# A two-layer spectral and expert-lookup kernel: the last token tile in halves, with buffers of its own and first place in the plan, and products of constants on TensorE in planned pauses

## Chip, cores, metric

The kernel runs on one core of one Trainium2 chip. The metric is the device time of one execution in microseconds, as the median of several runs.

## What is computed

The input is `x`, 2048 tokens of 512 features, in fp32. Two kinds of layer alternate, twice each, with a layer norm ahead of each and a residual around it:

```python
x = x + _A_ref(_layernorm(x), dft_seq_re, dft_seq_im, dft_hid_re, dft_hid_im)
x = x + _B_ref(_layernorm(x), w_q, k1, k2, u, v)
x = x + _A_ref(_layernorm(x), dft_seq_re, dft_seq_im, dft_hid_re, dft_hid_im)
x = x + _B_ref(_layernorm(x), w_q, k1, k2, u, v)

# _A_ref: real part of a Fourier transform over hidden and sequence
a = einsum("bsd,ed->bse", x, dft_hid_re); b = einsum("bsd,ed->bse", x, dft_hid_im)
y = einsum("ts,bse->bte", dft_seq_re, a) - einsum("ts,bse->bte", dft_seq_im, b)

# _B_ref: per token and head (32), two score lists of 16 keys, best two of each,
# best two of their four sums pick 2 of 256 experts
s1 = einsum("nhd,ed->nhe", q1, k1); s2 = einsum("nhd,ed->nhe", q2, k2)
g = softmax(top_s); act = gelu(einsum("nd,nhkd->nhk", xf, u[top_e]))
out = einsum("nhk,nhk,nhkd->nd", g, act, v[top_e])
```

## The kernel before

The tokens are 16 tiles of 128. Each fp32 operand is split into a high and a low part (`xh`, `xl` and so on), and a product is three matmuls, high by high, high by low and low by high. A layer is cut into nine units: seven of 256 tokens and two of 128 (tiles 14 and 15). `seq_unit` sums the sequence transform of a unit over all 16 tiles in four `acc` banks of PSUM: DMA of a block of the matrix (`raw`, L411), ACT makes its high part (`ch`, L415), DVE the low one (`cl`, L419), PE multiplies (L453); at the end ACT and DVE take the sums out (`pth` L478, `ptl` L481). `token_tile` then does all the rest for one tile:

- the hidden transform (`y`, L519, 24 matmuls of 512 columns), the residual (L526), the norm (L216 to L228, with one step on GpSimd, and L237), transposes (L541) and the split (`th` L548, `tl` L552);
- the scores of both key lists against all heads (L569, 24 matmuls, taken out by L575 into `sc`) and the products with all experts (L587, then the gelu on ACT and DVE, L592 to L607);
- the top-two search on DVE (L633 to L683, `tree32`, `eq`, `codes`, `tree16`), the gates (L697 to L737), which end in the small tile `q`;
- transposes of `q` (L746, L750), selection matrices (`lr`, L767, L773), products of these (L784), taken out by L791 into the gate matrix; four DMAs write it to DRAM (`gdr`, L806) and two read it back in another order (`gt`, L813);
- gates times activations (L815), transposes (L823), split (L827, L831), product with `v` (L843), residual (L847), store (L849).

The order of all this is not the order of the code. Every step is recorded as an `Op` with an engine, a cost in microseconds from a small table, the steps it comes after, the buffers it takes, and a priority; `Plan.run` places the ops one by one at the earliest time at which engine, inputs and buffers are free, and among those of the same earliest time takes the smallest priority. The kernel then issues the instructions in the order of planned start. The engines execute their own instructions in that fixed order, with semaphores for what they wait for. The choice within one engine is

```python
first = min(t for t, _ in can)
t, o = min((c for c in can if c[0] <= first + 1e-9), key=lambda c: (c[1].prio, c[1].n))
```

and a tile's priority is `prio = (0, layer, at if at < len(units) - 1 else -1, i)`, where `at` is the place of its unit in the layer. In the second layer the last units are tiles 12 and 13 (one unit) and then tile 15. Of the buffers, `sc`, `eq`, `top`, `qt` and `gt` exist once, `lr` four times; the gate matrix takes the `sc` buffer too. The end of the program is therefore the chain of tile 15, beside what is left of tiles 12 and 13.

## Time and profile before

| | |
|---|---|
| median of 3 runs | 1291.42 us (1289.96 to 1292.18) |
| profiled execution | 1293.34 us, span of its instructions 1291.6 us |
| TensorE busy | 1240.4 us, 96% of the span |
| VectorE busy | 991.7 us, 77% |
| ScalarE busy | 468.5 us, 36% |
| mean granted TensorE clock | 0.986 |

The span counts from the first instruction to the last. A matmul's length in the timeline includes the time in which its columns run out of the array, so matmuls in a row overlap and the distance of their starts is what one costs. VectorE's instructions overlap a little as well where the next does not need the one before. "Idle before" names how long the engine had stood still and what it had waited for. The granted clock is TensorE's share of its full 2.4 GHz; the other level seen here is half of that, 1.2 GHz.

### The profile page before, as it was taken

The page shows a single profiled execution, that of the slowest core. Times are in us where ns is not written, and L with a number is a line of the kernel's source. Part 1 is how long each engine was busy: PE and PEld are TensorE (multiplying, and loading weights), DVE is VectorE, ACT ScalarE, POOL GpSimd, SP SyncE. Part 2 cuts the span into 40 slices and gives each one's busy share as a digit, 9 for nine tenths or more (in the row PEclk, how much of TensorE's full clock was granted, in tenths as well). Part 3 has the DMA queues.
Part 4 walks back from the last instruction along what each step waited for, and adds up shares of the span by engine and source line. Part 5 has one row for each costly group of instructions (what it writes and reads, how often), then busy time and mean ns, then how long its engine had stood idle before and what let it go on. Part 6 is the DMA issues. An engine that isn't in the chain of part 4 may idle for free.

```text
span 1291.6 us, 20342 instructions
## 1 busy us (share of the span) xinstructions
PE 1240.4 (96%) x7648; PEld 1026.8 (80%) x7648; DVE 991.7 (77%) x2226; ACT 468.5 (36%) x967; POOL 46.0 (4%) x71
## 2 busy tenths in 40 slices
PE   7999999999999999999999999999999999999972
PEld 6877778777788778899889887878878887888951
DVE  7899997888898959578883498684957669495774
ACT  6522244333333433243562343332333333332421
POOL 2010000000000000000000000000000000000000
PEclk9999999999999999999999999999999999999985
DMA  7866640322232332413454024242241414224012
GB/s 218 261 197 214 188 155 26 90 69 56 73 82 66 88 84 58 114 36 98 120 140 131 25 55 111 49 115 58 65 107 41 115 50 105 59 68 104 18 17 33
DMA packets 228291, 121.42 MB, mean 94 GB/s; under 512 B 140640, under 2 KB 206688, under 8 KB 228192
## 3 DMA queue, kind: packets, MB, share of 16 engines
q1 hardware_dynamic: 228192, 120.12, 34.8%
q8 instruction: 60, 0.98, 0.3%
q14 instruction: 39, 0.32, 0.1%
HBM read 107.50 MB, written 12.58 MB: 93 GB/s over the span
## 4 chain that ended last, share of the span: by engine, by line
PE 55%; DVE 19%; DMA 4%; issue 3%; ACT 2%; SPq 2%; POOL 0%; DVEq 0%; ACTq 0%
PE acc L453 24%; PE bank L569 11%; PE bank L519 10%; PE bank L843 3%; DVE cl L419 3%; DVE eq L624 2%; PE bank L587 2%; DMA gt<-gdr 2%; PE bank L453 2%; DMA gdr<-sc 2%; DVE lr L767 1%; DVE eq L656 1%; SPq L806 1%; DVE tmp L648 1%; DVE eq L672 1%
## 5 line engine op out<-in xcount | busy, mean ns | idle before, releaser
L453 PE MATMUL acc<-ch,xh 128*128 128x512 f32 (+1 forms) x1088 | 414.9, 381 | 8.0 <-ACT xh L244 7.8
L453 PE MATMUL acc<-cl,xh 128*128 128x512 f32 (+1 forms) x1088 | 404.7, 372 | 0.0
L453 PE MATMUL acc<-ch,xl 128*128 128x512 f32 (+1 forms) x1088 | 404.5, 372 | 0.0
L415 ACT CAST ch<-raw 128x512 fp32r<-128x512 f32 x256 | 158.6, 620 | 273.3 <-PE acc L453 242.4
L453 PEld LDWEIGHTS acc<-ch,xh 128*128 128x128 f32 x1088 | 205.7, 189 | 41.1 <-ACT xh L244 7.8
L453 PEld LDWEIGHTS acc<-cl,xh 128*128 128x128 f32 x1088 | 205.4, 189 | 36.4
L453 PEld LDWEIGHTS acc<-ch,xl 128*128 128x128 f32 x1088 | 205.9, 189 | 32.4 <-DVE xl L245 0.5
L419 DVE TENSOR_TENSOR cl<-raw,ch 128x512 fp32r<-128x512 f32 x256 | 174.9, 687 | 32.0 <-ACT ch L415 31.2
L569 PE MATMUL bank<-wh,tok 128*128 128x512 f32 x512 | 165.6, 394 | 1.0 <-ACT tok L548 0.7
L569 PEld LDWEIGHTS bank<-wh,tok 128*128 128x128 f32 x512 | 97.2, 190 | 22.4 <-ACT tok L548 1.1
L519 PE MATMUL bank<-dh,pth 128*128 128x512 f32 x256 | 101.3, 396 | 0.3 <-ACT sc L791 0.3
L519 PE MATMUL bank<-dh,ptl 128*128 128x512 f32 x256 | 100.0, 391 | 0.8 <-DVE ptl L481 0.8
L569 PE MATMUL bank<-wl,tok 128*128 128x512 f32 x256 | 100.6, 393 | 0.0
L519 PE MATMUL bank<-dl,pth 128*128 128x512 f32 x256 | 99.8, 390 | 0.0
L767 DVE TENSOR_TENSOR lr<-iota,qt 128x1024 f16<-128x1024 f16 x128 | 83.5, 685 | 17.0 <-ACT qt L750 16.9
L225 POOL TENSOR_TENSOR stats<-stats,half 128x1 f32<-128x1 f32 x64 | 44.7, 702 | 1193.7 <-DVE stats L222 1189.1
L633 DVE TENSOR_TENSOR tmp<-sc 128x512 f32<-128x512 f32 x32 | 22.0, 688 | 75.1 <-ACT sc L575 75.1
L624 DVE TENSOR_TENSOR eq<-sc,val 128x1024 f16<-128x1024 f32 x64 | 78.3, 1223 | 1.5
L575 ACT COPY sc<-bank 128x512 f32<-128x512 f32 x64 | 36.2, 590 | 112.1 <-PE bank L569 55.5
L478 ACT CAST pth<-acc 128x512 fp32r<-128x512 f32 x62 | 36.0, 586 | 91.1 <-PE acc L453 89.2
L481 DVE TENSOR_TENSOR ptl<-acc,pth 128x512 fp32r<-128x512 f32 x62 | 42.3, 687 | 33.0 <-ACT pth L478 33.0
L656 DVE TENSOR_TENSOR eq<-eq 128x512 f16<-128x512 f16 (+2 forms) x192 | 59.3, 309 | 1.6
(113 smaller groups left out, 1677.5 us busy)
## 6 DMA issues: line engine op xcount, KB each, us to landing
raw<-in_cseq SPq DMA_DIRECT2D x224, 256.0 KB, 2.8
wr<-in_wq SPq DMA_DIRECT2D x32, 512.0 KB, 3.9
raw<-in_ctile SPq DMA_DIRECT2D x32, 256.0 KB, 2.9
wr<-in_x SPq DMA_DIRECT2D x16, 256.0 KB, 3.8
row<-in_x SPq DMA_DIRECT2D x16, 256.0 KB, 3.3
gdr<-sc SPq DMA_DIRECT2D x128, 32.0 KB, 2.2
gt<-gdr SPq DMA_DIRECT2D x64, 64.0 KB, 2.9
x2d<-row SPq DMA_DIRECT2D x16, 256.0 KB, 2.1
```

Of the source, the lines that this page charges most:

```text
L225: nc.gpsimd.tensor_tensor(st[:, 1:2], st[:, 1:2], half, op=ALU.pow)
L415: nc.scalar.copy(t[1], t[0])
L419: nc.vector.tensor_sub(t[2], t[0], as32(t[1]))
L453: nc.tensor.matmul(target(d), w[:, s, d * P:(d + 1) * P], moving(s % per, part), start=(s == 0 and k == 0 and d % blocks == 0), stop=(s == ...
L481: nc.vector.tensor_sub(view(1, k, ds), acc[k], as32(view(0, k, ds)))
L519: nc.tensor.matmul(t["y"], w[:, k, c, t0:t0 + P], r[:, c, k, :], start=(k == 0 and c == 0 and m == 0), stop=(k == KD - 1 and c == 1 and m ...
L569: nc.tensor.matmul(t["pc", hf], w[:, k, :], r[:, k, hf], start=(m == 0), stop=(m == 3 * KD - 1))
L575: nc.scalar.copy(t["sc"][:, :, hf, :], t["pc", hf].rearrange("p h e -> p e h"))
L624: nc.vector.tensor_tensor(t["eq"], flat("sc"), t["val"][:, rank_][:, None, :].to_broadcast([P, E, 64]), op=ALU.is_equal)
L656: nc.vector.tensor_max(t["eq"][:, :m], t["eq"][:, :m], t["eq"][:, m:2 * m])
L767: nc.vector.tensor_tensor(t["m", hf, r], io2, row_of(r, hf), op=ALU.is_equal)
L843: nc.tensor.matmul(t["po"], w[:, k, :], r[:, k, :], start=(m == 0), stop=(m == 5))
```

## The change

For the unit of the last tile of layer two (priority `FINAL`) the plan is made with another rule: an op of it is taken first if it can start at most 0.14 us after the earliest. The tile itself is cut in halves: the hidden transform by columns (two of 256), with its own residual and statistics each; the norm's application half on ACT and half on DVE; transposes and split in halves; the scores' matmuls with the high part first, so that they begin with the first half; the top-two search for one key list at a time; the selection products, the gate matrix and its DMAs in halves. Its buffers for `qt`, the selection matrices, the gate matrix and `gt` come from the `raw`, `ch` and `cl` buffers of the sequence transform. The stores of the two tiles before it are planned behind its read of the gate matrix. Its product with `v` is issued in two parts. For all tiles the low part of the scores is multiplied last, and in all units of 128 tokens the hidden transform multiplies the high parts first. At the beginning 16 products of two constant tiles are issued on TensorE (`FILL0`), and behind the last matmul of the sequence transform as many as fit by the plan's costs into each planned pause of over 1 us; nobody reads their results.

```diff
+
+FINAL = (0, 1, -2)
+SLACK = 0.14
+
+
+def HALVED(layer, at):
+    return layer == 1 and at == NCH + NSC * (TPC - 1) - 1
+
+
+FILL0 = 16
...
+                    keen = [c[0] for c in can if c[1].prio[:3] == FINAL and c[0] <= first + SLACK]
+                    first = min(keen, default=first)
                     t, o = min((c for c in can if c[0] <= first + 1e-9), key=lambda c: (c[1].prio, c[1].n))
                     if best is None or t < best[0]:
...
+        fine = prio[:3] == FINAL
...
+        if units[n][1] is None:
+            steps = [(k, (0, 1, 2)) for k in range(KD)]
+        else:
+
+            steps = [(k, (0, 1)) for k in range(KD)] + [(k, (2,)) for k in range(KD)]
+        wide = [slice(0, D)] if not fine else [slice(0, D // 2), slice(D // 2, D)]
...
+                a = op("PE", 2 * len(ms) * (MM512 if nc_ == D else MM256), f, [pready[layer, n][k][2 in ms], a] + dft_done,
+                       take=[hb] if z == 0 else [], behind=[a_row],
+                       last=[phold[layer, n]] if z == len(steps) - 1 else [], prio=prio)
...
+            b = op("DVE", dve(nc_), f_add, [a, a_row], last=[hb], prio=prio)
+            if fine:
+                bn_done.append(op("DVE", dve(nc_), f_bn(cs), [b], take=[] if bn_done else [hbn], prio=prio))
+
+        if fine:
+            a = ln_rest(lambda: t["bn"].rearrange("p a b -> p (a b)"), hbn, i, bn_done, prio)
...
+                cs = slice(k.start * P, k.stop * P)
+                if z == 0:
+                    ln_apply(t["xn"][:, cs], t["row"][:, cs], i)
+                else:
+                    nc.vector.tensor_scalar(t["xn"][:, cs], t["row"][:, cs], stats[:, i, 1:2], stats[:, i, 2:3],
+                                            op0=ALU.mult, op1=ALU.add)
...
+            def f_pch(hf=hf, ks=ks[0]):
+                if ks.start == 0:
+                    t["pc", hf] = bank([P, H, E])
+                for k in range(ks.start, ks.stop):
+                    for r in (wh, wl):
+                        nc.tensor.matmul(t["pc", hf], t["th"][:, k, :], r[:, k, hf], start=(k == 0 and r is wh), stop=False)
+
+            def f_pcl(hf=hf):
                 for k in range(KD):
-                    for w, r in ((t["th"], wh), (t["th"], wl), (t["tl"], wh)):
-                        nc.tensor.matmul(t["pc", hf], w[:, k, :], r[:, k, hf], start=(m == 0), stop=(m == 3 * KD - 1))
-                        m += 1
+                    nc.tensor.matmul(t["pc", hf], t["tl"][:, k, :], wh[:, k, hf], start=False, stop=(k == KD - 1))
...
+            if fine:
+                for z, k in enumerate(ks):
+                    a_pe = op("PE", 2 * (k.stop - k.start) * MM512, lambda f=f_pch, hf=hf, k=k: f(hf, k), [a_th[z], a_pe],
+                              take=[] if z else [hb], prio=prio)
+                a_pe = op("PE", KD * MM512, f_pcl, a_tl + [a_pe], prio=prio)
...
+        halved = HALVED(layer, at)
+        cuts = [(slice(f, f + 1), slice(f * H, (f + 1) * H), 32) for f in range(2)] if halved else [(slice(0, 2), slice(0, 64), 64)]
...
+            a = tree32(0, after)
+            a = codes([op("DVE", dve(16 * w), eq(0), a, prio=prio)])
+            a = tree16(key1, a)
...
+        a_val, a_key = [], []
+        for z, (fs, cols, w) in enumerate(cuts):
+            x, y = chain(z, fs, cols, w, [sc_parts[z]] if halved else sc_parts, prio + (z,) if halved else prio)
+            a_val += x
+            a_key += y
...
+        hb, hqt = Hold("bank"), Hold("raw" if fine else "qt")
...
+        soon = (0, 1, -1, i) if layer and at == len(units) - 2 else prio
...
+                    t["m", hf, r] = piece((16, E, 4), ("ch", "cl")[r], F16) if fine else work([P, 16, E, 4], F16, "lr")
                     nc.vector.tensor_tensor(t["m", hf, r], io2, row_of(r, hf), op=ALU.is_equal)
...
+                hls.append(Hold("lr") if not fine else hls[-1] if r else Hold("c"))
+                a = op("DVE", dve(1024, 2), f_m, [a_qt], take=[] if fine and r else hls[-1:], prio=soon)
...
+            made.append(op("DVE", dve(1024, 2), f_w, [a], last=[hqt] if hf else [], prio=soon))
+        hgs, hbs = [Hold("raw"), Hold("raw")] if fine else [Hold("sc")] * 2, [Hold("bank") for _ in range(2)]
...
+        if fine:
+            pe = [op("PE", 16 * MMG + 0.15, lambda hf=hf: f_blocks((hf,)), [made[hf]], take=hbs[hf:hf + 1],
+                     last=hls[2 * hf:2 * hf + 1], prio=prio) for hf in range(2)]
...
+            evac.append(op("ACT", act(512), f_gs(hf), [pe[hf]] + evac, take=hgs[hf:hf + 1] if fine or not hf else [],
+                           last=hbs[hf:hf + 1], prio=prio))
...
+        hd, hgt = Hold("gdr"), Hold("raw" if fine else "gt")
...
+        for z, gr in enumerate([slice(0, 8), slice(8, 16)] if fine else [slice(0, 16)]):
+            for k in range(4):
+                def f_out(z=z, gr=gr, k=k):
+                    if z == 0 and k == 0:
+                        t["gdr"] = dram.tile([2, E, 4, 16, E], F32, name="gdr", bufs=BUFS["gdr"])
+                    gs = t["gs", z] if fine else t["gs"]
+                    nc.sync.dma_start(t["gdr"][:, :, k, gr].rearrange("j e g f -> (j e) g f"), gs[k::4, :, k, :])
+                moves.append(op("SP", 0.3, f_out, evac[z:z + 1] if fine else evac[1:], behind=moves[:1],
+                                take=[] if moves else [hd], last=[hgs[z]], prio=prio, lag=2.4))
...
+                    t["gt"] = piece((E, E)) if fine else work([P, E, E], F32, "gt")
...
+        if fine:
+            a_ph = op("PE", 4 * MM512, f_poh, [a_ph], take=[hb], prio=prio)
+            a = op("PE", 2 * MM512, f_pol, [a, a_ph], last=[hpp], prio=prio)
...
+            if at == len(units) - 1:
+                for o in stores[-2:]:
+                    o.behind.extend(back)
+            stores.append(op("SP", load(256), lambda: nc.sync.dma_start(out[i * P:(i + 1) * P, :], t["row"]), [a],
+                             last=[hrow], prio=prio, lag=2.3))
...
+    def fill(at):
+        if "tile" not in spare:
+            spare["tile"] = psum.tile([P, D], F32, name="bank" if at == 0 else "acc", bufs=4)
+        if at == 0:
+            nc.tensor.matmul(spare["tile"], ident16, iota.rearrange("p e h -> p (e h)"), start=True, stop=True)
+        else:
+            nc.tensor.matmul(spare["tile"], dh[:, 0, 0, :P], dh[:, 0, 0, :], start=True, stop=True)
+
+    free = 0.0
+    for o in order:
+        if o.engine == "PE":
+            gap = o.start - free
+            if free == 0.0:
+                for _ in range(FILL0):
+                    fill(0)
+                spare.clear()
+            elif free >= seq_last.start and gap > 1.0:
+                for _ in range(int((gap - 0.4) / MM512)):
+                    fill(1)
+            free = o.start + o.us
         o.fn()
```

TensorE, from the last tile's hidden-dimension product to the first key products; before (`L519` is that product, `L746` the transposes of the keys `q`, `L541` those of the normalised tile, `L569` the key products):

```order
L519 MATMUL bank<-dh,ptl 128x512
L746 LDWEIGHTS q
L746 MATMUL bank<-ident_79,q 128x128
...
L541 MATMUL bank<-identf,tok 128x128 x4
L569 MATMUL bank<-wh,tok 128x512
L569 MATMUL bank<-wl,tok 128x512
```

The same place in the changed kernel and on to the last selection products (`L558`, `L607`, `L637`, `L668`, `L854`, `L944` and `L967` do what L519, L541, L569, L587, L746, L823 and L843 did; `L1047` are the products of constants):

```order
L558 MATMUL bank<-dh,ptl 128x256 x8
L1047 MATMUL acc<-dh 128x512 x11
L607 MATMUL bank<-identf,tok 128x128 x4
...
L668 MATMUL bank<-uh,tok 128x256
L1047 MATMUL acc<-dh 128x512 x44
L854 LDWEIGHTS q
...
L944 MATMUL bank<-identf,act 128x128 x2
L1047 MATMUL acc<-dh 128x512 x5
...
L967 MATMUL bank<-vh,pl 128x512 x2
L1047 MATMUL acc<-dh 128x512 x22
L944 MATMUL bank<-identf,act 128x128 x2
L1047 MATMUL acc<-dh 128x512 x3
```

Eighty-five constant products stand in the tail in five places (the 11, 44, 5, 22 and 3 above), and the transposes of tile 13's keys now come behind those of the last tile. The last three tiles' output products stand at the end as before, tile 12, tile 13, tile 15.

SyncE, all DMAs of the tail; before (`gdr` is the DRAM tile that reorders the gate matrix, 13552, 13746 and 13830 belong to tiles 12, 13 and 15; `out` are the stores of the rows):

```order
L806 DMA gdr_13552<-sc_13537 32x16x16 x4
L813 DMA gt_13586<-gdr_13552 64x16x16 x2
L849 DMA out_0<-row_12869 128x512
L806 DMA gdr_13746<-sc_13737 32x16x16 x4
L813 DMA gt_13778<-gdr_13746 64x16x16 x2
L806 DMA gdr_13830<-sc_13822 32x16x16 x4
L849 DMA out_0<-row_12876 128x512
L813 DMA gt_13846<-gdr_13830 64x16x16 x2
L849 DMA out_0<-row_13427 128x512
```

and changed (13582, 13888 and 13938 belong to tiles 12, 13 and 15):

```order
L926 DMA gdr_13582<-sc_13564 32x16x16 x4
L934 DMA gt_13624<-gdr_13582 64x16x16 x2
L926 DMA gdr_13888<-sc_13876 32x16x16 x4
L926 DMA gdr_13938<-raw_13916 32x8x16 x4
L926 DMA gdr_13938<-raw_13950 32x8x16 x4
L934 DMA gt_13961<-gdr_13888 64x16x16 x2
L934 DMA raw_13964<-gdr_13938 64x16x16 x2
L983 DMA out_0<-row_12886 128x512
L983 DMA out_0<-row_12893 128x512
L983 DMA out_0<-row_13445 128x512
```

The last tile's four writes have become eight of half the size and stand directly behind tile 13's; its two reads stand ahead of the stores of tiles 12 and 13, where they stood behind both.

VectorE, the top-two search of the last tile; before, whole (`sc` are the scores, `tmp`, `val` and `eq` the steps of the search, `L831` to `L847` other tiles' work):

```order
L633 TENSOR_TENSOR tmp<-sc 128x512
L648 TENSOR_TENSOR tmp<-tmp 128x256
L648 TENSOR_TENSOR tmp<-tmp 128x128
L648 TENSOR_TENSOR val<-tmp 128x64
L831 TENSOR_TENSOR pl<-bank,ph 128x256
L624 TENSOR_TENSOR eq<-sc,val 128x1024
L604 TENSOR_TENSOR act<-act 128x256
L672 TENSOR_TENSOR eq<-eq,iota 128x1024
L847 TENSOR_TENSOR row<-row,bank 128x512
```

and changed, from tile 13's selection matrices (`L877`, `L883`) on:

```order
L877 TENSOR_TENSOR lr<-iota,qt 128x1024
L727 TENSOR_TENSOR tmp<-sc 128x8x32
L734 TENSOR_TENSOR tmp<-tmp 128x4x32
L734 TENSOR_TENSOR tmp<-tmp 128x2x32
L734 TENSOR_TENSOR val<-tmp 128x32
L721 TENSOR_TENSOR eq<-sc,val 128x16x32
L761 TENSOR_TENSOR eq<-eq,iota 128x16x32
L743 TENSOR_TENSOR eq<-eq 128x8x32
L727 TENSOR_TENSOR tmp<-sc 128x8x32
L743 TENSOR_TENSOR eq<-eq 128x4x32
L734 TENSOR_TENSOR tmp<-tmp 128x4x32
```

Seven operations of the first key half stand alone, from the eighth on the two halves alternate, and the other tiles' operations have gone out of the search.

## Rows read from the trace of the kernel before

**Rows 1.** Windows of the tail: busy time by engine (instructions), granted clock, DMA share, GB/s.
```profile
1239.70:1251.00 11.30, 9.23 (x32) 7.06 (x33) 4.97 (x9) 2.47 (x4) 0.55 (x1) 0.70 0.15 15
...
1263.00:1291.60 28.60, 8.95 (x51) 5.58 (x51) 9.74 (x28) 4.32 (x11) 0.00 (x0) 0.56 0.23 38
```

**Rows 2.** Timeline of the start: start, length, engine, line, operation [idle before <- releaser].
```profile
1.33 0.63 DVE L178 CAST ident<-identf 128x128 f16<-128x128 f32 x1 [1.33 <-POOL identf L176]
...
8.57 0.80 PE L453 MATMUL acc<-ch,xl 128*128 128x512 f32 x1
...
11.70 0.16 DVE L228 SCALAR_TENSOR_TENSOR stats<-stats 128x1 f32<-128x1 f32 x1 [0.35 <-POOL stats L225]
...
12.15 0.49 PE L453 MATMUL acc<-ch,xh 128*128 128x512 f32 x1
...
12.91 0.62 ACT L415 CAST ch<-raw 128x512 fp32r<-128x512 f32 x1 [2.82 <-PE acc L453]
...
15.66 0.39 PE L453 MATMUL acc<-ch,xh 128*128 128x512 f32 x1
...
15.89 0.39 PE L453 MATMUL acc<-ch,xl 128*128 128x512 f32 x1
```

**Rows 3.** Timeline of the tail, TensorE.
```profile
1237.01 0.39 PE L519 MATMUL bank<-dh,ptl 128*128 128x512 f32 x1
...
1243.17 0.79 PE L569 MATMUL bank<-wh,tok 128*128 128x512 f32 x1 [0.68 <-ACT tok L548]
...
1250.74 0.39 PE L569 MATMUL bank<-wh,tok 128*128 128x512 f32 x1
...
1254.71 0.40 PE L843 MATMUL bank<-vh,pl 128*128 128x512 f32 x1
...
1277.66 0.63 PE L843 MATMUL bank<-vh,pl 128*128 128x512 f32 x1
```

**Rows 4.** Windows of the tail after TensorE's last products, columns as in rows 1.
```profile
1258.00:1259.00 1.00, 0.00 (x0) 0.00 (x0) 0.97 (x2) 0.00 (x0) 0.00 (x0) 0.61 0.13 45
...
1282.00:1284.00 2.00, 0.21 (x1) 0.25 (x2) 0.43 (x1) 0.00 (x0) 0.00 (x0) 0.53 0.25 25
```

**Rows 5.** Timeline of the tail, VectorE.
```profile
1240.54 1.90 DVE L767 TENSOR_TENSOR lr<-iota,qt 128x1024 f16<-128x1024 f16 x3
...
1251.79 0.69 DVE L633 TENSOR_TENSOR tmp<-sc 128x512 f32<-128x512 f32 x1 [6.28 <-ACT sc L575]
...
1265.65 0.23 DVE L713 TENSOR_TENSOR q<-key,df 128x128 f16<-128x128 f16 x1
```

**Rows 6.** Groups by form, 1204 to 1292: count | busy us, mean ns | idle before.
```profile
L624 DVE TENSOR_TENSOR eq<-sc,val 128x1024 f16<-128x1024 f32 x6 | 7.3, 1221 | 0.1
...
L672 DVE TENSOR_TENSOR eq<-eq,iota 128x1024 f16<-128x1024 f16 x6 | 4.1, 685 | 0.0
...
L633 DVE TENSOR_TENSOR tmp<-sc 128x512 f32<-128x512 f32 x3 | 2.1, 689 | 11.1 <-ACT sc L575 11.1
...
L656 DVE TENSOR_TENSOR eq<-eq 128x512 f16<-128x512 f16 x6 | 2.5, 423 | 0.1
```

**Rows 7.** Timeline of the tail, SyncE's DMA issues.
```profile
1272.17 2.63 SPq L806 DMA_DIRECT2D gdr<-sc  x4
1279.04 0.34 SPq L849 DMA_DIRECT2D out<-row  x1
1279.61 1.32 SPq L813 DMA_DIRECT2D gt<-gdr  x2
```

**Rows 8.** Chain of waits at the end: start, length, what.
```profile
1266.14 2.19 DMA gdr<-sc
...
1269.17 4.40 DMA gt<-gdr
...
1280.27 2.85 DMA gt<-gdr
...
1284.91 2.94 PE bank L843 x6
```

More of the change, by code (lines that the diff above doesn't have):

```diff
@@ L211, in ln_stats, with f0, ln_rest @@
         bn, h = {}, Hold("bn")
+        def f0():
+            bn[0] = apool.tile([P, 2, 6], F32, name="bn", bufs=BUFS["bn"])
+            nc.vector.bn_stats(bn[0][:, 0], get())
+        a = op("DVE", dve(512), f0, after, take=[h], prio=prio)
+        return ln_rest(lambda: bn[0][:, 0], h, i, [a], prio)
+    def ln_rest(bn, h, i, after, prio):
         st = stats[:, i, :]
-        def f0():
-            bn[0] = apool.tile([P, 6], F32, name="bn", bufs=BUFS["bn"])
-            nc.vector.bn_stats(bn[0], get())
         def f1():
-            nc.vector.bn_aggr(st[:, 0:2], bn[0])
+            nc.vector.bn_aggr(st[:, 0:2], bn())
         def f2():
@@ L228, in f4 @@
             nc.vector.scalar_tensor_tensor(st[:, 2:3], st[:, 0:1], -1.0, st[:, 1:2], op0=ALU.mult, op1=ALU.mult)
-        a = op("DVE", dve(512), f0, after, take=[h], prio=prio)
-        a = op("DVE", 0.1, f1, [a], last=[h], prio=prio)
+        a = op("DVE", 0.1, f1, after, last=[h], prio=prio)
         a = op("DVE", 0.1, f2, [a], prio=prio)
@@ L511, in token_tile @@
         a = None
-        for k in range(KD):
-            def f(k=k):
-                if k == 0:
-                    t["y"] = bank([P, D])
-                pth, ptl = ptile[layer, n]
-                for c in range(2):
-                    for m, (w, r) in enumerate(((pth, dh), (pth, dl), (ptl, dh))):
-                        nc.tensor.matmul(t["y"], w[:, k, c, t0:t0 + P], r[:, c, k, :],
-                                         start=(k == 0 and c == 0 and m == 0),
-                                         stop=(k == KD - 1 and c == 1 and m == 2))
-            a = op("PE", 6 * MM512, f, [pready[layer, n][k], a] + dft_done, take=[hb] if k == 0 else [], behind=[a_row],
-                   last=[phold[layer, n]] if k == KD - 1 else [], prio=prio)
@@ new lines, in token_tile, with f_bn, f, f_add @@
+        wide = [slice(0, D)] if not fine else [slice(0, D // 2), slice(D // 2, D)]
+        hbn, bn_done = Hold("bn"), []
+        def f_bn(cs):
+            def f():
+                if "bn" not in t:
+                    t["bn"] = apool.tile([P, 2, 6], F32, name="bn", bufs=BUFS["bn"])
+                nc.vector.bn_stats(t["bn"][:, len(t["bns"])], t["row"][:, cs])
+                t["bns"].append(cs)
+            return f
+        for cs in wide:
+            hb, nc_ = Hold("bank"), cs.stop - cs.start
+            for z, (k, ms) in enumerate(steps):
+                def f(z=z, k=k, ms=ms, cs=cs):
+                    if z == 0:
+                        t["y", cs.start] = bank([P, cs.stop - cs.start])
+                    pth, ptl = ptile[layer, n]
+                    pairs = ((pth, dh), (pth, dl), (ptl, dh))
+                    for c in range(2):
+                        for m in ms:
+                            w, r = pairs[m]
+                            nc.tensor.matmul(t["y", cs.start], w[:, k, c, t0:t0 + P], r[:, c, k, cs],
+                                             start=(z == 0 and c == 0 and m == 0),
+                                             stop=(z == len(steps) - 1 and c == 1 and m == 2))
+                a = op("PE", 2 * len(ms) * (MM512 if nc_ == D else MM256), f, [pready[layer, n][k][2 in ms], a] + dft_done,
+                       take=[hb] if z == 0 else [], behind=[a_row],
+                       last=[phold[layer, n]] if z == len(steps) - 1 else [], prio=prio)
+            def f_add(cs=cs):
+                t["bns"] = t.get("bns", [])
+                nc.vector.tensor_add(t["row"][:, cs], t["y", cs.start], t["row"][:, cs])
+            b = op("DVE", dve(nc_), f_add, [a, a_row], last=[hb], prio=prio)
+            if fine:
+                bn_done.append(op("DVE", dve(nc_), f_bn(cs), [b], take=[] if bn_done else [hbn], prio=prio))
@@ L748, in f_qt @@
         def f_qt():
-            t["qt"] = work([P, 3, P], F16, "qt")
+            t["qt"] = piece((3, P), dtype=F16) if fine else work([P, 3, P], F16, "qt")
             nc.scalar.copy(t["qt"].rearrange("p r (q j) -> p r q j", q=16),
@@ L899, in spectral_peer_kernel @@
         mix(layer)
-    order = plan.run()
-    for o in sorted(order, key=lambda o: o.start):
+    order = sorted(plan.run(), key=lambda o: o.start)
+    spare = {}
+    def fill(at):
[3 more added lines that the diff above has]
+            nc.tensor.matmul(spare["tile"], ident16, iota.rearrange("p e h -> p (e h)"), start=True, stop=True)
+        else:
+            nc.tensor.matmul(spare["tile"], dh[:, 0, 0, :P], dh[:, 0, 0, :], start=True, stop=True)
[11 more added lines that the diff above has]
+            free = o.start + o.us
         o.fn()
```

262 lines of the change are left out of this document (139 added, 123 removed).

## Prediction

> **What bounds the kernel now.** I read the windows first, then the timeline of both ends, then the chain of waits. In between TensorE works without a pause worth counting, and this change puts no matmul there that was not there before; what it can move lies in the first 16 us and behind the last sequence matmul. The window from 1263 us to the end [rows 1] shows a stage in which no engine is the bound: TensorE is busy for 8.95 of 28.6 us at a granted clock of 0.56, VectorE for 9.74, ScalarE for 4.32. That is one serial chain, tile 15's, and its links are read from the timeline. TensorE ends the hidden transform at 1237.4 (1237.01 + 0.39) and does nothing but transposes until the first score matmul at 1243.17; the 24 score matmuls last to 1251.13 [rows 3]. VectorE searches from 1251.79 to `q` at 1265.88 [rows 5]. The gate matrix starts to leave at 1272.17; the read back, issued at 1279.61, stood behind tile 13's store at 1279.04 [rows 7] and lands at 1283.12, and from there 8.5 us remain, 2.94 of them the last six matmuls [rows 8].
>
> **The start.** The first matmuls run at half rate, though the profile puts the granted clock there at 1.00: from 8.57 to 12.15 eight steps take 3.58 us, while neighbours at 15.66 and 15.89 are 0.23 apart [rows 2]. The 16 new products need the identity, copied by 1.96 [rows 2]. At 0.45 for ten, as many as were slow, and 0.23 for six they take 5.9 us and end by 7.9, ahead of the second real matmul at 8.57 [rows 2], which waits for its data, so they hold up nothing. Eight steps at 0.23 take 1.8 us: 1.7 saved. Do the data follow? ScalarE's cast at 12.91 had waited 2.82 us for TensorE to free its buffer, and the statistics for the next tile were there at 11.70 [rows 2]; both allow about 1.5 us or more. I take 1.7, with 0 (the data don't follow, or the products run on past 8.57) and 1.9 as ends.
>
> **From the hidden transform to the scores.** The columns stay the same (48 matmuls of 256 for 24 of 512), and the high-first order of the small units only permutes them, so TensorE still ends near 1237.4. But one half's residual and statistics are done by then; the application is shared by two engines; two transposes and half a split suffice for the first score. Each 512-wide step becomes a 256-wide one, about 0.69 to 0.42 on VectorE by [rows 6]; with the queue of tile 13's small operations in between I take 1.3 us off the 5.8 (ends 0.5 and 2.0). The scores: 24 matmuls took 7.96 us because the first ten ran at half rate. The eleven constant products (2.5 us at 0.23) fill the pause up to about 1239.9, and a pause of 1 us is left. At full rate 24 cost 5.5: 2.4 off (lower end 0). Sum 3.7; the scores are in at 1248.1.
>
> **The search.** It took 14.1 us [rows 5] with tiles 12's and 13's operations inside; now these stand ahead or behind, and two half searches alternate. Three f16 operations that don't need one another take 1.90 [rows 5], where one is 0.685 long [rows 6]: 0.61 apiece, 0.08 less than alone. So a half costs 0.61 for each of its three 1024-wide fp32 steps (0.69 less 0.08), 0.34 for each of three f16 ones (0.42 less 0.08), and, by estimate from 0.34 at 256 elements downward, 0.8 for each of two fp32 trees and 0.57 for each of two f16 trees: 1.83 + 1.02 + 1.6 + 1.14 = 5.6, both 11.2. The first seven operations of the first half (1.9 of this) run while the second half of the scores is multiplied, as soon as tile 13's five selection operations are through. That leaves 9.3, plus seven gate operations of 0.1, 0.7 for the last four and 0.5 of stalls: 11.2 us, 2.9 off. At the other end each half step costs its whole length and a gap (7.8 a half, as in a chain of its own): 15.6 less 2.6, plus 1.4, is 14.4, or 0.3 lost. I take the first, because the order does alternate and the alternating steps don't need one another. Meanwhile 44 constant products take 44 x 0.23 = 10.0 us from about 1248.9; `q` comes at 1259.3, so they are just done and TensorE is at full rate.
>
> The Trainium skill speaks against halves here (VectorE: DVE Perf Modes, section "The TRN2 errata"): an operation from SBUF pays a fixed extra that lies between instructions, so many small ones pay it each; it advises 512 elements or more. By that rule the search is the 14.4 us above, and the end comes 3.2 us later than I forecast; the 0.61 of neighbours shows part of that extra hidden.
>
> **From `q` to the gate matrix read back.** Before, 1265.88 to 1283.12: 17.2 us. Now the second half of the gate matrix is in SBUF 5.7 us after `q` (was 6.3). On SyncE tile 13's four writes, whose products stand behind tile 15's transposes, go first: from 3.0 to 5.6 us after `q`, at 0.66 each [rows 7]. Then eight half writes. Half a write has no row: it lies between the 0.34 of a store with few pieces and the 0.66 of a whole one [rows 7]; I take 0.49, the middle, so 3.9 us, to 9.5. They land 2.2 later [rows 8]; two reads of 0.66, issued right then because no store stands ahead, go by 13.0; landing 2.9 to 4.4 [rows 8], I take 3.1: 16.1 us. That is 1.1 off; with the ends 0.34 and 0.66 for a write, 2.3 and -0.3.
>
> The Trainium skill (DMA: Bandwidth & Descriptors, "Rules for kernel authors") says to coalesce, as a transfer under 64 KB is mostly overhead. By it a half write costs a whole one, which is the -0.3 end.
>
> **To the end.** 8.5 us. At full rate the six matmuls cost 1.5 instead of 2.94 and the transposes 0.3 less; tile 13's six now stand right ahead and cost 0.2 of waiting. 1.5 off. Whether the rate is full is the open point. The last long run of constant products is 22 (5.0 us), planned from the plan's short DMA costs; by my times the pause it fills is 8.1 us, so TensorE stands for 3.1. Before, matmuls ended at 1255.1 and the clock fell within 1258 to 1259 (0.61 is a mean, so at about 1258.2); they ended at 1278.3 and it fell at about 1282.1, by the 0.53 of the window [rows 3, 4]: 3.1 and 3.8 us later. So it may just hold.
>
> **Sum.** 1.7 + 3.7 + 2.9 + 1.1 + 1.5 = 10.9 us off the profiled execution's 1293.34 (span 1291.6). That one is 1.9 above the median of 1291.42, from which I count: **1280.5 us**. A measurement of this kernel tells about 0.2% (2.6 us) from no change.
>
> **Rivals.**
> - *The clock falls in the last pause.* Then both sets of six matmuls, transposes and three constant products start at half rate: tile 13's six 1.4 us longer, the constants 0.6 past their wait, transposes 0.3 twice, with tile 15's partly at full rate again: 2.5 to 3.9 later, about 1283.4. For it: the two falls above sit at my 3.1. Against: a cheaper half write shortens the pause.
> - *The halves don't overlap.* Search 14.4 us, `q` 3.2 later; the 44 products end 3.7 before it, so the clock may fall too: 1284 to 1287. Against: the 0.61 steps.
> - *The start gives nothing*, the data being the bound: 1282.2. Against: the 2.82 us in which ScalarE waited for TensorE.
> - *The constant products run at half rate* and are in the way. If only the 44 do, they take 18.8 us, `q` is transposed 12 us later than forecast, and the gain is gone: 1292.5. If all after 1237 do (the scores 8.0 us, the 22 then 9.4), the end lies about 20 later: 1301, slower. It decides from about 43 products at 0.43 on. Against: matmuls in a row reached the full rate at both places seen here, and the fills are matmuls in a row.
> - *The change doesn't do what it says*: no, the order shows the halves, the buffers and the stores where the text puts them; only the sizes of the pauses are the plan's guess.
>
> **Numbers.** Forecast 0.50, clock falls 0.26, halves 0.12, no gain at the start 0.06, slow products 0.06 (half of it near 1292.5, half above). So faster 0.94, same 0.03, slower 0.03. Range: below, the forecast with cheap writes (1.2) and the better norm (0.7) gives 1278.6, less half a microsecond for run spread; above, the fallen clock on a slow half search or a 4.4 us landing, 1286.5.
>
> **What would show it.** The first real matmuls 0.23 apart, and TensorE's step at 15.89 some 1.7 earlier; score matmuls all 0.23 apart in a window at 1.00; search from the last score to `q` near 11 us; eight writes of about 0.5; reads ahead of the stores; last six matmuls in 1.5 us or in 2.9. It is wrong if matmuls behind the constant products start 0.43 apart, or if TensorE is still working on constants when `q` is ready.

## The result: 0.4% slower, and the profile after

The changed kernel takes 1296.51 us (median of 6 runs) beside 1291.61 for the kernel before: ratio 1.0037, 95% interval 1.0024 to 1.0050. The forecast was 1280.5, range some 1278 to 1286.5. The profiled execution took 1295.98 us, span 1294.1.

The page's first part, kernel after: 98% of the span on TensorE, where it was 96%.

```profile
PE 1274.1 (98%) x7773; PEld 1038.6 (80%) x7773; DVE 994.8 (77%) x2252; ACT 467.9 (36%) x968; POOL 45.6 (4%) x71
```

**Both ends became shorter, as intended.** Timeline of the start, kernel after (start, length, engine, line, operation, idle before): the constant products end ahead of the first real matmul, and from 8.58 on matmuls follow at full rate, which before began at 12.15 [rows 2].

```profile
5.71 1.24 PE L1045 MATMUL bank<-iota,ident 128*128 128x512 f16 x5
7.77 0.49 PE L470 MATMUL acc<-ch,xh 128*128 128x512 f32 x1 [0.82 <-ACT xh L261]
8.58 0.50 PE L470 MATMUL acc<-ch,xl 128*128 128x512 f32 x1 [0.31 <-DVE xl L262]
...
9.14 0.40 PE L470 MATMUL acc<-ch,xh 128*128 128x512 f32 x1
9.38 0.40 PE L470 MATMUL acc<-ch,xl 128*128 128x512 f32 x1
```

The tail's steps, each execution by its own timeline (us; the last column is an experiment told below):

| step | before | forecast | after | 544 bytes |
|---|---|---|---|---|
| hidden transform of tile 15 ends at | 1237.4 | 1235.7 | **1246.3** | 1236.0 |
| to the scores in SBUF | 14.4 | 10.7 | 10.7 | 10.3 |
| search, to `q` | 14.3 | 11.2 | 11.1 | 11.1 |
| to the gate matrix read back | 17.1 | 16.1 | 16.8 | 16.2 |
| to the end of the span | 8.4 | 7.0 | 9.3 | 8.3 |
| tail in all | 54.2 | 45.0 | 47.8 | 45.8 |

So the tail is 6.4 us shorter, the start is earlier, and yet tile 15's hidden transform ends 8.9 us later than before: **the loss lies in between**, where nothing was expected to change. Windows from 50 to 1225 us, before and then after (busy time of TensorE and its instructions, granted clock, DMA share, GB/s):

```profile
50.00:1225.00 1175.00, 1164.25 (x7244) 1.00 0.35 92
```
```profile
50.00:1225.00 1175.00, 1169.91 (x7166) 1.00 0.34 92
```

At the same granted clock of 1.00 and with 5.7 us less waiting, TensorE gets through 78 matmuls fewer. Each is slower. The chain of waits shows it in unbroken stretches (start, length, engine, tile, line, count), before and after, a hidden transform and a stretch of the sequence transform:

```profile
810.08 5.44 PE bank L519 x24
...
871.96 5.44 PE acc L453 x24
```
```profile
813.42 5.60 PE bank L558 x24
...
875.68 5.60 PE acc L470 x24
```

5.44/24 is 226.7 ns a matmul, 5.60/24 is 233.3: at 2.4 GHz 544 cycles for 512 columns, and 560. It holds from the first stretch to the last, in instructions that the change does not touch. Over the trace (60 to 1230 us) neighbours of 512 columns start 228.0 ns apart on average before and 233.1 after. 3841 such steps cost 19.6 us more; 5.7 less waiting, some 2.4 from faster 256-column matmuls (119.7 to 117.4 ns, about 1000 of them) and some 1.5 from the start leave about 10, beside the 8.9 seen.

In the tail, SyncE after:

```profile
1270.46 2.63 SPq L926 DMA_DIRECT2D gdr<-sc  x4
1273.14 6.40 SPq L926 DMA_DIRECT2D gdr<-raw  x8
1279.63 1.32 SPq L934 DMA_DIRECT2D gt<-gdr  x2
1281.18 1.29 SPq L934 DMA_DIRECT2D raw<-gdr  x2
```

Eight half writes took 6.40 us; four whole ones took 2.63 [rows 7]. And TensorE after, around the last pause, with two windows of it (busy time of PE, PEld, DVE, ACT, POOL, then the granted clock):

```profile
1274.76 5.17 PE L1047 MATMUL acc<-dh 128*128 128x512 f32 x22
1283.93 0.41 PE L944 MATMUL bank<-identf,act 128*128 128x128 f32 x2 [4.01 <-DVE act L936]
...
1285.03 0.63 PE L963 MATMUL bank<-vh,ph 128*128 128x512 f32 x1
1285.45 0.63 PE L963 MATMUL bank<-vl,ph 128*128 128x512 f32 x1
```
```profile
1280.00:1283.90 3.90, 0.00 (x0) 0.00 (x0) 0.43 (x1) 0.00 (x0) 0.00 (x0) 1.00 0.64 62
1284.70:1288.10 3.40, 3.40 (x10) 2.35 (x8) 1.03 (x3) 0.05 (x1) 0.00 (x0) 0.50 0.05 17
```

TensorE stands still for 4.01 us and goes on while the granted clock is still 1.00; from 1284.7 on the clock is 0.50, and tile 13's last six matmuls start 0.42 to 0.43 us apart.

### The profile page after: what moved, and what is told of

Its sections match the earlier page's. It is cut to its first block, busy times and chain, and to the rows that moved or that the text cites. A ratio compares the mean times of both kernels' runs of the same rounds, so it can differ in the third digit from the quotient of the medians.

```text
span 1294.1 us, 20619 instructions
## 1 busy us (share of the span) xinstructions
PE 1274.1 (98%) x7773; PEld 1038.6 (80%) x7773; DVE 994.8 (77%) x2252; ACT 467.9 (36%) x968; POOL 45.6 (4%) x71
## 4 chain that ended last, share of the span: by engine, by line
PE 85%; DVE 8%; DMA 2%; SPq 2%; issue 1%; ACT 1%; POOL 0%; DVEq 0%; ACTq 0%
PE acc L470 48%; PE bank L558 12%; PE bank L637 8%; PE bank L641 4%; PE bank L668 3%; PE bank L963 2%; PE bank L366 2%; SPq L926 1%; PE bank L893 1%; PE bank L470 1%; PE bank L607 1%; PE bank L967 1%; DVE cl L436 1%; DMA gt<-gdr 1%; DVE eq L721 1%
## 5 line engine op out<-in xcount | busy, mean ns | idle before, releaser
L558 PE MATMUL bank<-dh,pth 128*128 128x512 f32 (+1 forms) x264 | 103.4, 394 | 0.7 <-ACT pth L495 0.7
L558 PE MATMUL bank<-dl,pth 128*128 128x512 f32 (+1 forms) x264 | 101.9, 388 | 0.0
L637 PE MATMUL bank<-wh,tok 128*128 128x512 f32 x256 | 101.6, 397 | 0.0
L637 PE MATMUL bank<-wl,tok 128*128 128x512 f32 x256 | 101.3, 396 | 0.0
L727 DVE TENSOR_TENSOR tmp<-sc 128x512 f32<-128x512 f32 (+1 forms) x66 | 44.4, 672 | 69.6 <-ACT sc L646 68.9
L558 PE MATMUL bank<-dh,ptl 128*128 128x512 f32 (+1 forms) x264 | 96.9, 389 | 0.0
L877 DVE TENSOR_TENSOR lr<-iota,qt 128x1024 f16<-128x1024 f16 x124 | 80.9, 685 | 19.1 <-ACT qt L858 19.0
L721 DVE TENSOR_TENSOR eq<-sc,val 128x1024 f16<-128x1024 f32 (+1 forms) x66 | 78.6, 1191 | 1.5
L641 PE MATMUL bank<-wh,tok 128*128 128x512 f32 x256 | 70.1, 396 | 0.0
L743 DVE TENSOR_TENSOR eq<-eq 128x256 f16<-128x256 f16 (+3 forms) x198 | 60.2, 304 | 1.6
```

The lines of the kernel that those rows point to most:

```text
L558: nc.tensor.matmul(t["y", cs.start], w[:, k, c, t0:t0 + P], r[:, c, k, cs], start=(z == 0 and c == 0 and m == 0), stop=(z == len(steps) - ...
L637: nc.tensor.matmul(t["pc", hf], t["th"][:, k, :], r[:, k, hf], start=(k == 0 and r is wh), stop=False)
L641: nc.tensor.matmul(t["pc", hf], t["tl"][:, k, :], wh[:, k, hf], start=False, stop=(k == KD - 1))
L721: nc.vector.tensor_tensor(t["eq"][:, :, cols], flat("sc")[:, :, cols], val(rank_, cols), op=ALU.is_equal)
L727: nc.vector.tensor_max(t["tmp"][:, :, cols], flat("sc")[:, :8, cols], flat("sc")[:, 8:, cols])
L743: nc.vector.tensor_max(s[:, :m], s[:, :m], s[:, m:2 * m])
```

## The experiments

**Theory.** The compiled program tells where each buffer lies. Buffers start on multiples of 32 bytes, one behind the other. The change makes the buffer of the norm's statistics, `bn`, `[P, 2, 6]` in place of `[P, 6]`: 48 bytes per partition for 24, so 64 for 32 in the layout. Everything allocated behind it (`ch`, `cl`, `pth`, `ptl`, `tok`, `ph`, `pl`) moves by 32 bytes; the constants (`xh`, `dh`, `wh`, `vh`) lie ahead of it and stay. Rivals: the constant products at the start, the new order of the score products, or the program's length set the pace.

**The kernel before with that buffer alone.**

```diff
-bn[0] = apool.tile([P, 6], F32, name="bn", bufs=BUFS["bn"])
+bn[0] = apool.tile([P, 12], F32, name="bn", bufs=BUFS["bn"])[:, :6]
```

> The kernel before, whose statistics buffer alone is made 48 bytes instead of 24, so that everything behind it moves by 32 bytes. Theory of the 64-byte start: 512-column matmuls 233 ns apart from the first to the last, and a time of 1300 to 1304 us (1291.6 plus the 9 to 12 us that the middle of the changed kernel lost; at most 4352 x 5.2 ns = 22 us if no pause takes any of it up). Rivals (constant products, order, program's length): 227 ns and 1291.6 us, no difference.

Measured: 1304.47 us, ratio 1.0096 (1.0082 to 1.0110), so about 12 us lost by an allocation that nothing reads. The chain of waits of this kernel:

```profile
752.31 5.60 PE acc L453 x24
...
817.73 5.59 PE bank L519 x24
```

That is the pace of the changed kernel, without any other part of the change. The cause is the layout.

**The changed kernel without the first constants.**

```diff
-FILL0 = 16
+FILL0 = 0
```

> The changed kernel without the 16 constant products at the start, its buffers still at odd multiples of 32 bytes. Theory of the 64-byte start: 233 ns in the middle all the same, the first matmuls at half rate again, so 1.5 to 2 us slower than the changed kernel, about 1298.3 us. Rival that those products set the pace of what follows: 227 ns in the middle and about 1288 us.

Measured: 1297.76 us, ratio 1.0042 (1.0028 to 1.0055); the middle stays at 233 ns (first row below, chain of waits), and the start (the last two rows, timeline) is at half rate again; the row between them is SyncE's eight half writes. Its first `pth` comes at 52.3 us, with the constants at 49.2. The rival falls. What the constants are worth at the end, 1.3 us by the medians, is not resolved: without them tile 15's hidden transform ends 4.1 us later (1250.4), but in this execution the clock held in the last pause and none of the eight half writes stood longer than the others, so its tail took 45.0 us where it was 47.8.

```profile
817.34 5.60 PE bank L558 x24
```
```profile
1277.21 5.25 SPq L926 DMA_DIRECT2D gdr<-raw  x8
```
```profile
9.64 0.63 PE L470 MATMUL acc<-cl,xh 128*128 128x512 f32 x1
10.06 0.63 PE L470 MATMUL acc<-ch,xh 128*128 128x512 f32 x1
```

**The changed kernel, `bn` of 96 bytes**, at both places where it is allocated.

```diff
-apool.tile([P, 2, 6], F32, name="bn", bufs=BUFS["bn"])
+apool.tile([P, 4, 6], F32, name="bn", bufs=BUFS["bn"])
```

> Theory: the one buffer of the norm's statistics grew from 24 to 48 bytes per partition, and with it every buffer behind it (ch, cl, pth, ptl, tok, ph, pl) went from a multiple of 64 bytes to an odd multiple of 32; TensorE then loads its weights from there and paces 512-column fp32r matmuls at 233 ns where they stood at 227. This kernel is the changed one with 96 bytes for that buffer, which puts the others back on multiples of 64 and changes nothing else. The theory expects 227 ns between neighbours in the sequence transform, the hidden transform of tile 15 to end about 9 to 10 us earlier than 1246.2, and 1286 to 1288 us. Rivals (the constant products at the start, the new order of the score products, or the program's length set the pace): 233 ns and 1296.5 us as in the changed kernel.

Measured: 1290.42 us, ratio 0.9990 (0.9981 to 1.0000). Better by 6 us, but short of the expectation, and the chain says where: the sequence transform went to 5.51/24 = 229.6 ns, the hidden transform stayed at 233.

```profile
811.30 5.61 PE bank L558 x24
...
873.06 5.51 PE acc L470 x24
```

The two differ in one thing: in the first the shifted buffer is the moving operand (`ch` against `xh`), in the second it is the weights (`pth` against `dh`).

**`bn` of 160 bytes**: the others on multiples of 128 again.

```diff
-apool.tile([P, 2, 6], F32, name="bn", bufs=BUFS["bn"])
+apool.tile([P, 40], F32, name="bn", bufs=BUFS["bn"])[:, :12].rearrange("p (a b) -> p a b", b=6)
```

> The changed kernel with 160 bytes for the statistics buffer, which puts everything behind it at the kernel before's place plus 128 bytes, so on multiples of 128 again; with 96 bytes it stood on odd multiples of 64. Theory: TensorE keeps 227 ns only where both its operands start at a multiple of 128 bytes. It expects 227 to 228 ns in the hidden transform and the scores too (233 with 96 bytes), the hidden transform of tile 15 to end between 1235 and 1237 us, and 1281 to 1286 us. Rival (a multiple of 64 is enough, and the 233 ns left in those products come from the new order of the score products or from constants before them): 233 ns there and 1290 us as with 96 bytes.

A miss: 1295.77 us, ratio 1.0024 (1.0014 to 1.0033), 5.60/24 and 5.59/24 in the chain.

```profile
813.31 5.60 PE bank L558 x24
...
875.37 5.59 PE acc L470 x24
```

So it is not enough that both operands start on multiples of 128. The next kernel ran beside it.

**Sixteen pairs of starts, constants only.** The whole body is this, with `w` and `m` by their offsets:

```python
for a in (0, 32, 64, 96):
    for b in (0, 32, 64, 96):
        for _ in range(100):
            ps = psum.tile([P, D], F32, name="ps", bufs=4)
            nc.tensor.matmul(ps[:, :cols], w[a][:, :P], m[b][:, :cols], start=True, stop=True)
```

> This kernel computes nothing of the reference but multiplies constants: 100 fp32r matmuls in a row for each of 16 pairs of a weights buffer and a moving buffer that start 0, 32, 64 or 96 bytes behind a multiple of 128, first with 512 columns, then with 256. Theory of the start address: 22.7 us for a hundred of 512 columns where both start at 0, 23.3 where the weights start at 32, 64 or 96 or the moving operand at 32 or 96, about 23.0 for the moving operand at 64 (as the sequence transform showed with 96 bytes); with 256 columns about 12.0 at 0 and 11.7 elsewhere. Rival (the pace hangs on what ran before, or on changing operands, and not on where one operand starts): the same time for all 16 pairs.

Mean distance of starts in its one execution (ns, steps 21 to 99 of each hundred, 512 columns):

```
weights at   moving at 0      32      64      96
   0            233.4   234.3   233.3   233.3
  32            233.3   232.3   234.3   233.3
  64            228.9   233.3   232.3   234.3
  96            233.3   228.9   233.3   233.3
```

Neither the theory nor its rival expected this, but the table is nearly constant along its diagonals. In this kernel the two buffers labelled 0 lie 2176 bytes apart; each step of the moving label adds 2080 to that, each step of the weights' label takes 544 off. What fields of one pace share is the distance between the two starts: it is 64 modulo 512 in both fields with 228.9. It is 0 modulo 256 or 512 in none.

**The sweep of that distance.** One `w`, and moving buffers of 2080 bytes one behind the other, so 32 bytes further each:

```diff
-nc.tensor.matmul(ps[:, :cols], w[a][:, :P], m[b][:, :cols], start=True, stop=True)
+nc.tensor.matmul(ps[:, :cols], w, t[:, :cols], start=True, stop=True)
```

> Constants alone again: one weights buffer, and 17 moving buffers that start 0, 32, 64 and so on to 480 and then 512 bytes behind it, counted modulo 512, then one moving buffer read 4, 8, 16, 32 and 64 bytes in; 100 fp32r matmuls of 512 columns for each, then of 256. Theory from the sixteen pairs: the pace of TensorE goes by the distance between the starts of the two operands modulo 512 bytes. It expects, with 512 columns, 226.7 ns at 0 and again at 512, 228.9 at 64, 232 to 234 at 32, 96 to 224, 384, 448 and 480 (as in the pairs and in the kernels so far), and no value yet for 256 to 352 and for 4 to 16. Rival (what counts is where each operand starts by itself): no such curve, and 512 unlike 0.

Groups of this kernel by form (count, busy us, mean ns of one, idle before). The moving buffers b, c, e, f, g, i and k lie 32, 64, 128, 160, 192, 256 and 320 bytes behind the weights, counted modulo 512, and q a multiple of 512:

```profile
L182 PE MATMUL ps<-m_f,w 128*128 128x512 f32 x100 | 23.6, 396 | 0.0
...
L182 PE MATMUL ps<-m_b,w 128*128 128x512 f32 x100 | 23.5, 395 | 0.0
...
L182 PE MATMUL ps<-m_e,w 128*128 128x512 f32 x100 | 23.5, 395 | 0.0
...
L182 PE MATMUL ps<-m_c,w 128*128 128x512 f32 x100 | 23.1, 391 | 0.0
L182 PE MATMUL ps<-m_k,w 128*128 128x512 f32 x100 | 23.1, 391 | 0.0
L182 PE MATMUL ps<-m_i,w 128*128 128x512 f32 x100 | 22.8, 389 | 0.0
L182 PE MATMUL ps<-m_q,w 128*128 128x512 f32 x100 | 22.8, 389 | 0.0
...
L182 PE MATMUL ps<-m_q,w 128*128 128x256 f32 x100 | 12.2, 283 | 0.0
...
L182 PE MATMUL ps<-m_g,w 128*128 128x256 f32 x100 | 11.5, 276 | 0.0
```

With 512 columns the settled distance of starts is 226.7 ns at 0, 256 and 512, 228.9 at 64 and 320, and 233.3 to 234.3 at the other multiples of 32. The theory holds with a period of 256 bytes, half of what was expected. With 256 columns the order is another: 120.0 at 0, 113.3 at 192 and 448. The kernels fall into line (distance of the moving start behind the weights' start modulo 256, and mean step in ns between 60 and 1230 us):

| kernel | sequence | hidden | scores |
|---|---|---|---|
| before | 0: 228.0 | 0: 227.9 | 0: 227.1 |
| after; before with 48 bytes | 32: 233.1; 233.0 | 224: 233.1; 233.3 | 224: 233.3; 233.3 |
| after, 96 bytes | 64: 229.6 | 192: 233.1 | 192: 233.1 |
| after, 160 bytes | 128: 232.5 | 128: 232.6 | 128: 232.7 |
| after, 544 bytes | 0: 227.9 | 0: 227.9 | 0: 227.3 |

At a distance of 128 the kernels show 232.5 to 232.7, the pairs 232.3 to 233.4 and the sweep 233.3; at the others the three agree within 1.3 ns.

**`bn` of 544 bytes**: the changed kernel with the distances of the kernel before.

```diff
-apool.tile([P, 2, 6], F32, name="bn", bufs=BUFS["bn"])
+apool.tile([P, 136], F32, name="bn", bufs=BUFS["bn"])[:, :12].rearrange("p (a b) -> p a b", b=6)
```

> The changed kernel with 544 bytes for the statistics buffer: everything behind it stands 512 bytes behind its place in the kernel before, so at the same distance modulo 512 from the constants. Theory of the distance modulo 512: 227 ns in sequence transform, hidden transform and scores, the hidden transform of tile 15 to end between 1235 and 1237 us, and 1280 to 1286 us. Rival (the change slows these matmuls by something beside the addresses): 231 ns or more in some of them and 1289 us or more.

Measured: 1285.82 us, ratio 0.9947 (0.9935 to 0.9958). The chain of waits is back at the pace of before, and the hidden transform of tile 15 ends at 1236.0.

```profile
809.16 5.44 PE bank L558 x24
...
870.49 5.44 PE acc L470 x24
```

**Constants in the last pause**, on the kernel with 96 bytes.

```diff
-for _ in range(int((gap - 0.4) / MM512)):
+count = int((gap - 0.4) / MM512)
+for _ in range(39 if count == 22 else count):
```

> The first of these kernels (statistics buffer of 96 bytes) with 39 constant products in the last pause in place of 22, which is 3.9 us more of them and fills the 4.0 us in which TensorE stood still before tile 13's last transposes. Theory that the clock fell in that pause and cost time: tile 13's last six matmuls go 0.23 us apart in place of 0.43, and the end comes 1.2 to 2 us before that of the kernel with 22. Rival (the end is set by transfers, not by these matmuls, or the products run past the arrival of the gate matrix): no gain, or up to 0.5 us lost.

Measured: 1290.76 us beside 1290.42, ratio 0.9988 (0.9979 to 0.9997). In the trace the clock held and the time from the landing of tile 15's read back to the end fell from 8.8 to 7.9 us; in the medians, whose runs scatter by some 6 us, nothing shows.

**Whole writes of the last gate matrix** (on 160 bytes).

```diff
-enumerate([slice(0, 8), slice(8, 16)] if fine else [slice(0, 16)])
+enumerate([slice(0, 16)])
...
-    t["gs", hf] = piece((8, 4, E))
+    gs = apool.tile([P, KD, 2, T], F32R, name="pth")
```

> The kernel with 160 bytes, whose last tile's gate matrix leaves in four whole writes from one buffer in place of eight half writes from two; the order on all other queues is the same. Theory that a half write occupies SyncE as long as a whole one (0.66 us) and that one of the eight stood 1.1 us longer: the last read back is issued 2.3 to 2.9 us earlier behind the search's end, and the kernel is 2 to 2.5 us faster than with halves. Rival (the first halves' head start pays for them): no gain, or up to 1.3 us lost.

Measured: 1291.77 us beside 1295.77 with halves, ratio to before 1.0000 (0.9991 to 1.0010). From the gate matrix in SBUF to the issue of tile 15's first read it was 5.1 us (7.0 with halves), so 1.9 of the 2.3 to 2.9 expected; one of the four writes stood longer here too. Another 1.5 us came from the clock, which held in the shorter pause (7.75 us from landing to end for 9.25); what is left of the 4.0 between the medians is not accounted for.

```profile
1273.91 3.43 SPq L926 DMA_DIRECT2D gdr<-pth  x4
1277.51 1.32 SPq L934 DMA_DIRECT2D gt<-gdr  x2
1278.99 1.29 SPq L934 DMA_DIRECT2D raw<-gdr  x2
```

**The same with 29 constants.**

```diff
-for _ in range(int((gap - 0.4) / MM512)):
+for _ in range((lambda c: {22: 29}.get(c, c))(int((gap - 0.4) / MM512))):
```

> The kernel with whole writes and 29 constant products in the last pause in place of 22. Theory that TensorE's clock falls in what is left of the pause: tile 13's last six matmuls 0.23 us apart and another 1 to 1.2 us off the end. Rival (with the shorter pause the clock holds anyway, or the seven products run into tile 13's transposes): 0 to 0.5 us lost.

Measured: 1292.29 us, ratio 0.9998 (0.9990 to 1.0007): the rival. With whole writes 22 are enough in this execution (7.75 us from landing to end, 7.73 with 29).

**Both mended: 544 bytes and whole writes** (the edits of those two kernels together).

> The same with four whole writes of the last gate matrix in place of eight halves. By the pair with 160 bytes, whose tail was 3.3 us shorter with whole writes, 3 to 4 us faster than the kernel with 544 bytes alone, so 1277 to 1282 us. Rival (that gain was scatter between runs): no difference.

Measured: **1281.55 us, ratio 0.9921 (0.9908 to 0.9934)**, faster than both kernels. TensorE in its last pause, at full rate behind 1.52 us of standing still:

```profile
1269.90 0.41 PE L944 MATMUL bank<-identf,act 128*128 128x128 f32 x2 [1.52 <-DVE act L936]
...
1271.11 0.40 PE L963 MATMUL bank<-vl,ph 128*128 128x512 f32 x1
1271.34 0.41 PE L963 MATMUL bank<-vh,ph 128*128 128x512 f32 x1
```

**`ph` and `pl` put at distance 0 as well.**

```diff
-work([P, E, E], F32, "gt")
+work([P, 288], F32, "gt")[:, :N].rearrange("p (a b) -> p a b", b=E)
```

> The same again, with 1152 in place of 1024 bytes for the buffer ahead of ph and pl, so that these two stand at distance 0 modulo 512 from vh and vl, which they did not in the kernel before either (128 bytes; 232 ns there). Theory of the distance: 227 in place of 232 ns for the matmuls of the expert output, 192 x 5 ns = 1 us at most, of which about half may show. Rival (those matmuls are short groups that never settle): 230 ns or more still, and no difference.

Measured: 1281.72 us, ratio 0.9919 (0.9908 to 0.9931), no difference. These matmuls come in groups of six: their mean step went from 232.3 to 230.3 ns (high parts) and from 232.4 to 229.0 (low), not to 227. In this execution the clock fell in the last pause, and landing to end took 9.3 us for 7.8: the price of that fall is 1.5 us.

## Why the prediction was wrong

**The step that failed** is the first one: "In between TensorE works without a pause worth counting, and this change puts no matmul there that was not there before", and with it "so TensorE still ends near 1237.4". Both were read from the order of instructions, and indeed no matmul was added in between (7773 for 7648 in all: 101 constants, and 24 more by the halves of tile 15's hidden transform). But the statement that adds a second half to `bn` moved all buffers behind it by 32 bytes, and some 3800 steps between matmuls got 5 ns longer each. It was counted at nothing because it was not looked at: an allocation was read as a name and not as a place. With the distance restored and nothing else altered the kernel is at 1285.82 us, within the range given; from 1.0037 to 0.9947 the size of that buffer alone made some 11 to 12 us (in the two profiled executions 10.3 up to the end of the hidden transform and 2.0 in the tail). None of the five rivals had it. The result's side, slower, was forecast with 0.03 and from another mechanism (constant products at half rate), which did not occur: 44 constants took 10.2 us, as forecast (10.0).

**Term by term**, read from the execution with 544 bytes, whose middle is that of before. *Start* 1.7: the hidden transform ends 1.4 earlier, with all that differs up to there, so the start's own share is not isolated (in the three kernels with 160 bytes this end lies between 1244.7 and 1246.4). *Hidden transform to scores* 3.7: 4.1; the score matmuls ran at the full rate. *Search* 2.9: 3.2; it takes 11.06 us in the changed kernel, 11.2 was forecast, and the two halves do hide each other's gaps: in the timeline after, an operation of 0.69 us costs 0.72 where the next one needs it and 0.60 where the next belongs to the other half.

```profile
1255.51 0.69 DVE L721 TENSOR_TENSOR eq<-sc,val 128x512 f16<-128x512 f32 x1
1256.23 0.42 DVE L761 TENSOR_TENSOR eq<-eq,iota 128x512 f16<-128x512 f16 x1
...
1258.54 0.69 DVE L721 TENSOR_TENSOR eq<-sc,val 128x512 f16<-128x512 f32 x1
1259.14 0.68 DVE L774 SCALAR_TENSOR_TENSOR sc<-eq,sc 128x512 f32<-128x512 f16 x1
```

The Trainium skill (VectorE: DVE Perf Modes, section "The TRN2 errata") says that each operation from SBUF pays a fixed extra that lies between instructions; the prediction read this as the 14.4 of its other end. The trace shows part of the extra hidden between two independent chains, and not that there is none: operations of 32 elements still start 0.10 to 0.11 us apart.

*`q` to the read back* 1.1: 0.9, by two errors that nearly cancel: the writes ended 1.5 us later behind `q` than forecast, and from there to the landing it was 5.1 us where 6.6 was taken. The half write was mis-sized: I took 0.49 us, it measured 0.66, a whole one's time, and one of the eight stood longer (in the changed kernel by 1.1: 6.40 us for eight, where 3.9 was forecast). The -0.3 end, at which a half costs a whole, was the right one for the writes. The Trainium skill (DMA: Bandwidth & Descriptors, "Rules for kernel authors") says that a transfer under 64 KB is mostly overhead, and the trace agrees: a half write of 16 KB takes the 0.66 us of a whole one of 32 KB on SyncE and lands 1.9 us after its issue, the whole one 2.2. *To the end* 1.5: 0.2, mis-sized as well, though the clock held there. Where it holds, the time from the landing of tile 15's read back to the end is 7.7 to 8.3 us, so 0.2 to 0.7 off and not 1.5: tile 13's six matmuls and its split stand ahead of tile 15's, whose last six start 2.4 us after the landing (with 544 bytes and whole writes), 1.8 before [rows 8]; 0.2 had been taken for that. So the end no longer hangs on the transfer that the prediction counted from. The last transfer in the chain of waits is tile 13's read back (into `gt`; tile 15's goes into `raw`); in the changed kernel:

```profile
1280.28 2.99 DMA gt<-gdr
```

From that landing to the end it is 9.1 to 9.3 us in the six kernels whose clock held in the last pause and 10.7 to 10.9 in the four where it fell, while tile 15's read back lands 1.0 to 2.1 us later.

Sum of these: 9.8 beside 10.9 forecast, from one execution to one execution. Between medians the gain is less, 6.8 us by the ratio (5.4 to 8.4): the profiled execution of before (1293.34) lies 1.5 above the median of 1291.88 in that comparison, and that of 544 bytes (1283.56) 2.3 below its own. What in the scatter of runs makes up the difference stays open.

**The rivals.** *The clock falls in the last pause* did happen in the changed kernel (0.50 from 1284.7 to 1288.1), just behind 4.0 us of standing still; before, it fell after 3.1 and 3.8. Its price was some 1.5 us (10.7 to 10.9 for 9.1 to 9.3, above), not 2.5 to 3.9, because only tile 13's six matmuls, constants and transposes met it; tile 15's six ran at 1.00 again. *The halves don't overlap* fell by the 11.06 us. *The start gives nothing* fell by the timeline of the start and the first `pth`, which comes 3.1 us earlier with the constants than without; the medians do not show that gain.

## What to carry to other kernels

An edit that makes one buffer larger moves every buffer behind it, so compare the addresses of TensorE's operands before and after, not only the order of instructions. Where a kernel is bound by fp32r matmuls of 512 columns, lay weights and moving operand out so that their starts lie a multiple of 256 bytes apart: 512 bytes of unused space in `bn` gave this kernel back 0.9%. And when a profile shows the same instructions at the same granted clock with matmuls another time apart, suspect the layout before the schedule.

## What the runs showed of the hardware

- The step of fp32r matmuls in a row went by the distance of the two operands' starts modulo 256 bytes: 226.7 ns at 0, 228.9 at 64, 232.3 to 234.3 at other multiples of 32 (512 columns); a moving start 4 bytes off gave 236.7. With 256 columns it ran from 113.3 (192) to 120.0 (0, 96), so 0 is the best for one width and not for the other. Which part of the chip makes it was not tried, nor whether a matmul's own weights count or those loaded beside it. The Trainium skill (SBUF — State Buffer, "Operand start alignment") asks only for a start at a multiple of the element's size and says that this is about legality, not speed; all starts here keep that rule.
- Short groups do not reach the settled pace: six in a row at distance 0 stood at 229.0 to 230.3 ns on average.
- On SyncE a DMA of half a gate matrix block took the same 0.66 us to issue as a whole one. In nine of the ten kernels with the changed tail one of the last tile's writes, half or whole, stood longer, 1.09 to 1.76 us (below, the changed kernel); in the one without the first constants none of the eight did. What makes it stays open.

```profile
1274.47 1.76 SPq L926 DMA_DIRECT2D gdr<-raw  x1
```
